# A fused attention and gMLP block on one core: w_in loaded twice in shifted row order in place of copies across partitions, with new task lists

## The chip, the core and the metric

The kernel runs on one core of a Trainium2 chip. The core has TensorE (PE in the profile; PEld is its loading of weights), VectorE (DVE), ScalarE (ACT), GpSimd (POOL) and SyncE (SP), which here only issues DMAs. The metric is the time of one execution on the device in microseconds (us). A profile shows one such execution; its span runs from the first to the last instruction, and the execution's own time is a little longer.

## The reference

Two residual blocks follow each other on 2048 tokens of 448 features, in bf16:

```python
h = x + _A_ref(_layernorm(x, axis=-1), A_wqkv, A_wo)
h2 = h + _B_ref(_layernorm(h, axis=-1), B_w_in, B_w_sp, B_b_sp, B_w_out)
```

`_A_ref` is local attention: 16 heads of 28 features; each token attends to 8 tokens, itself and those 2, 4, ... 14 positions before it. `_B_ref` is a gMLP: `z = gelu(x @ w_in)` with 1792 columns, of which the first half is z1 and the normalised second half z2; `g = w_sp @ z2 + b_sp` mixes over the tokens with a 2048 x 2048 matrix, and the output is `(z1 * g) @ w_out`.

## The kernel before

**Layout.** Tokens are cut into 16 blocks of 128. Block u and block u + 8 make unit u (u from 0 to 7) and are worked on together: after the layer norm they lie interleaved in one buffer of the ring `tring`, and a transpose puts them into `xh` as 7 chunks of 128 partitions. Partitions 0 to 63 of a chunk hold 64 features of block u, and partitions 64 to 127 the same 64 features of block u + 8. A matmul of 64 rows on the lower half and one on the upper half run side by side on PE, one for each half of the tokens. So every weight matrix that multiplies `xh` (wq, wk, wv, w_in) is needed as 7 chunks of 64 rows on both halves of the partitions.

**Where the weights come from.** A DMA on all 128 partitions puts the even chunks on one half and the odd chunks on the other. The function `cross` (used for wv and, as `cpw0`, `cpw1`, for w_in) then copies what each half lacks from the other half, on VectorE or ScalarE (the helper `copy`, lines 641 and 643). `BLK` (line 25) says for each half of the partitions which chunk of features lies in which place. wq and wk are copied into a padded form by the tasks `cpq...` and `cpk...`: 8 copies for q, 4 for k (`cpk` + first head group j, half h, parity q).

**w_in.** `ld_win(z)` loads half z of its columns (z = 1 for z2, 0 for z1) by three DMAs (256, 128 and 64 rows), and two `cross` copies follow. The readers are `mmz2_u_k` (line 984) and `mmz1_ch_f` (line 1028).

**Stages.** Layer norm 1 for each unit: `bn1_b` (statistics), `rs1_u` (reciprocal root, on POOL by lines 646 and 647 or on ScalarE by lines 668 and 669), `nrm1_b` (line 676), then a transpose, for units 7, 6, 5 on PE (`tT1_u`, line 692, with its copy `ev1_u`), for the others by a DMA (`tD1_u`, line 683). Then the projections `mmq`/`mmk` (line 783, ended by the evictions `evq`/`evk`; the first number is the stretch of tokens) and `mmv` (line 823, `evv`). Attention goes in 9 tiles i from 8 down to 0: `mml` (scores, line 858, four tasks a tile), `exp`, `mask`, `mmr` (row sums, line 886), `ln` and `rex` (reciprocal), `mmo` (line 911, four tasks), `ot`. Then `mmy_u` (line 964), the residual `h_u`, layer norm 2 (`bn2`, `rs2`, `nrm2`, and the transposes `tD2_u` by DMA), `mmz2`, its gelu `ge`, `bn3`, `ag3`, `rs3` and `nrm3` (line 1014); `mmz1` with the gelu `gz1`. The spatial matmuls `g` (line 1064) read z2 and w_sp transposed by the DMAs `wsp0_b` and `wsp1_b`; `wo` (line 1093) and stores end the kernel.

**What sets the order.** The order is written out in the file as `SEQ`, one tuple for each of SP, POOL, DVE, ACT and PE, of positions in the order in which the tasks were added. `Planner.replay` walks through these lists with estimated durations, gives out PSUM banks (eight; most matmul tasks take two, a pair, until the eviction has read them) and other buffers, and emits each engine's instructions in the order of its list. Each engine then runs its list in order and waits where something isn't ready. All DMAs but a few of the first are issued from SP's list, in order too: a transpose that waits for its input holds back what stands behind it. Each `wsp` DMA also waits until the one before it has landed (`chain`).

Decoded from the positions, PE's list up to the spatial matmuls is (`mml8_00..11` are the tasks 00, 01, 10 and 11):

```
f0 tT1_7 tT1_6 mmq3_0 mmv8 mmv7 mmq2_0 mmk3_2 mmk2_2 mmk2_0 mmk3_0 mmq3_2 mmq2_2 tT1_5 mml8_00..01 mml7_00 mml8_10..11
mml7_01 mmv6 mmq1_0 mmk1_2 mml7_10..11 mmk1_0 mmq1_2 mmr7 mmo7_0..3 mmv5 mmv2 mmr8 mmo8_0..3 mmk0_0 mmk0_2 mml6_00..01
mml5_00..01 mmq0_2 mml5_10 mml6_10 mml5_11 mml6_11 mmq0_0 mmk0_1 mmq0_3 mmr5 mmo5_0..1 mmr6 mmo5_2..3 mmq0_1 mmk0_3
mmy7 mmo6_0..3 mml4_00..11 mmv4 mml3_00..11 mmy6 mmr4 mmo4_0..3 mmv3 mml2_00..01 mmy5 mml2_10..11 mmr3 mmy4 mmo3_0..2
mmr2 mmo3_3 mmv0 mml1_00..11 mmv1 mmy3 mmr1 mmo2_0..3 mml0_00..11 mmz2_7_1 mmy2 mmo1_0..1 mmr0 mmo1_2..3 mmz2_7_0
mmz2_4_0 mmo0_0..3 mmy1 mmy0 mmz2_5_1 mmz2_5_0 mmz2_4_1 mmz1_1_0 mmz2_6_0 ... mmz1_0_1 mmz1_0_4 g0_2_0 g0_1_0 g0_0_0
```

`f0` is 15 matmuls on constants that warm PE up.

Of the kernel before, what the change touches and what calls it, by code (L numbers as in the profile page):

```python
# [23 lines left out]
DMA_T = {1: range(5), 2: range(8)}  # L24
BLK = ((0, 2, 4, 6, 1, 3, 5), (1, 3, 5, 0, 2, 4, 6))
# [353 lines left out]
def bass_sequential_preLN__sliding_local_dilated__mixer_gmlp__prompt_kernel(  # L379
# [18 lines left out]
    with contextlib.ExitStack() as top:  # L398
# [340 lines left out]

        t_cp = {}  # L740
        for p in "kq":
            for j in range(2 if p == "q" else 1):
                nh = 8 if p == "q" else 16
                for n, (h, q) in enumerate(((0, 0), (0, 1), (1, 0), (1, 1))):
                    tk = []
# [418 lines left out]
```

## Time and profile before

| | before |
|---|---|
| time, median of 3 runs | 242.88 us (242.75 to 243.28) |
| profiled execution | 242.73 us |
| its span | 240.9 us |
| PE busy | 233.1 us, 97% of the span |
| DVE, ACT, POOL busy | 140.3, 96.1, 26.9 us |
| DMA | 20.01 MB in 54628 packets |
| granted clock of PE | 1.00 throughout |

Busy time is the union of an engine's instructions in the profile. Matmuls are pipelined, so the length of one matmul is longer than the distance to the next; the price of a task on PE is best read as the distance between the starts of two tasks. In a row of the timeline the bracket gives how long the engine was idle before it and what released it; "issue" means that nothing in the profile was waited for. A row of the windows gives, for each engine, the busy time and in brackets the number of instructions.

### The profile page before, as it was taken

How to read it: one execution, taken by the hardware profiler on the slowest of the kernel's cores; microseconds unless marked ns; L12 is line 12 of the kernel's file. 1: busy time of each engine (PE TensorE's matmuls, PEld its weight loads, DVE VectorE, ACT ScalarE, POOL GpSimd, SP SyncE). 2: the span in 40 equal slices, each digit the busy share in tenths (PEclk: the TensorE clock that was granted, in tenths of full speed). 3: DMA queues.
4: the chain of work that ended last, by engine and by line, in shares of the span. 5: the costliest groups of instructions: out<-in, count | busy, mean ns of one | idle time of the engine just before them, and what ended most of it. 6: DMA issues, size and time to landing. Idle time of an engine off the chain costs nothing.

```text
span 240.9 us, 6695 instructions
## 1 busy us (share of the span) xinstructions
PE 233.1 (97%) x3009; PEld 119.9 (50%) x3019; DVE 140.3 (58%) x280; ACT 96.1 (40%) x113; POOL 26.9 (11%) x66
## 2 busy tenths in 40 slices
PE   7898999999999999999999999999999999999995
PEld 2486865456554544554444444444444444444453
DVE  5999959378999899788810050253101436554443
ACT  2996988889899947764730000000000000000000
POOL 4062000002014321304600000000000000000000
PEclk9999999999999999999999999999999999999999
DMA  7949575574213557987632733350000000010122
GB/s 213 337 106 103 112 125 95 97 127 53 44 22 77 109 85 174 169 133 117 141 76 58 174 68 65 85 46 0 0 0 3 0 0 19 20 60 0 38 93 78
DMA packets 54628, 20.01 MB, mean 83 GB/s; under 512 B 46792, under 2 KB 54472, under 8 KB 54600
## 3 DMA queue, kind: packets, MB, share of 16 engines
q1 hardware_dynamic: 53496, 18.67, 39.6%
q10 hardware_dynamic: 1104, 0.92, 1.3%
q8 instruction: 23, 0.38, 0.7%
q14 instruction: 5, 0.04, 0.1%
HBM read 6.37 MB, written 1.84 MB: 34 GB/s over the span
## 4 chain that ended last, share of the span: by engine, by line
PE 88%; DVE 5%; DMA 2%; issue 1%; POOL 1%; ACT 1%; SPq 0%
PE psum L1064 40%; PE psum L783 11%; PE psum L1093 9%; PE psum L984 8%; PE psum L964 5%; PE psum L823 5%; PE psum L1028 4%; PE psum L858 2%; PE psum L911 2%; DMA x_tm<-in_A_x_dram 2%; DVE z2p L1014 2%; PE psum L886 1%; DVE st L1000 1%; DVE tring L676 1%; POOL rs L647 1%
## 5 line engine op out<-in xcount | busy, mean ns | idle before, releaser
L1073 DVE TENSOR_TENSOR ub<-psum,reg 128x512 bf16<-128x512 f32 x28 | 18.9, 687 | 68.7 <-PE psum L1064 66.4
L1064 PE MATMUL psum<-reg,z2p 128*128 128x512 bf16 x220 | 49.4, 379 | 0.2
L1064 PE MATMUL psum<-wspT_lo,z2p 128*128 128x512 bf16 x218 | 48.5, 379 | 0.4 <-DVE z2p L1014 0.2
L1064 PEld LDWEIGHTS psum<-wspT_lo,z2p 128*128 128x128 bf16 x224 | 21.8, 98 | 26.6 <-issue 0.4
L1064 PEld LDWEIGHTS psum<-reg,z2p 128*128 128x128 bf16 x224 | 21.9, 98 | 26.2
L783 PE MATMUL psum<-xh,reg 64*128 64x128 bf16 (+2 forms) x448 | 26.0, 270 | 0.2
L1093 PE MATMUL psum<-reg 128*128 128x448 bf16 (+2 forms) x119 | 22.2, 341 | 0.1
L984 PE MATMUL psum<-w_in,xh 64*128 64x448 bf16 x224 | 22.2, 349 | 0.0
L1028 PE MATMUL psum<-xh,w_in 64*128 64x512 bf16 x196 | 21.8, 376 | 0.0
L641 ACT ACTIVATE reg<-psum 128x896 bf16<-128x896 f32 (+2 forms) x25 | 20.0, 844 | 1.9 <-PE psum L783 1.0
L783 PEld LDWEIGHTS psum<-xh,reg 64*128 64x128 bf16 x448 | 16.8, 94 | 7.8 <-issue 0.8
L656 DVE BATCH_NORM_STATS2 st<-x_tm 128x6 f32<-128x448 bf16 x32 | 19.6, 612 | 1.4 <-DMA x_tm<-in_A_x_dram 1.2
L1000 DVE BATCH_NORM_STATS2 st<-z2p 128x6 f32<-128x448 bf16 x32 | 17.5, 611 | 3.1 <-ACT z2p L994 3.1
L870 ACT ACTIVATE reg<-psum 128x928 bf16<-128x928 f32 x18 | 16.2, 939 | 4.1 <-PE psum L858 4.1
L646 POOL TENSOR_SCALAR rs<-mv 128x2 f32<-128x2 f32 x19 | 7.5, 393 | 88.4 <-DVE mv L657 70.2
L1038 ACT ACTIVATE reg<-psum 128x1024 bf16<-128x1024 f32 x14 | 13.6, 1029 | 8.0 <-PE psum L1028 8.0
L1093 PEld LDWEIGHTS psum<-reg 128*128 128x128 bf16 x119 | 11.4, 98 | 10.4
L994 ACT ACTIVATE z2p<-psum 128x896 bf16<-128x896 f32 x16 | 14.2, 916 | 5.6 <-PE psum L984 5.6
L1103 DVE TENSOR_TENSOR tring<-psum,x_tm 128x448 bf16<-128x448 f32 (+2 forms) x17 | 10.1, 596 | 10.2 <-PE psum L1093 10.1
L984 PEld LDWEIGHTS psum<-w_in,xh 64*128 64x128 bf16 x224 | 10.6, 94 | 10.4 <-issue 0.4
L929 DVE TENSOR_TENSOR reg<-psum,reg 128x912 bf16<-128x912 f32 x9 | 11.1, 1235 | 7.2 <-ACT reg L921 6.6
L1028 PEld LDWEIGHTS psum<-xh,w_in 64*128 64x128 bf16 x196 | 9.5, 94 | 11.5
(63 smaller groups left out, 205.9 us busy)
## 6 DMA issues: line engine op xcount, KB each, us to landing
x_tm<-in_A_x_dram SPq DMA_DIRECT2D x15, 112.0 KB, 4.2
out_dram<-tring SPq DMA_DIRECT2D x15, 112.0 KB, 1.7
w_in<-in_B_w_in_dram SPq DMA_DIRECT2D x2, 448.0 KB, 4.5
reg<-in_B_w_out_dram SPq DMA_DIRECT2D x1, 784.0 KB, 6.0
z2p<-in_A_wqkv_dram ACTq DMA_DIRECT2D x2, 336.0 KB, 4.5
reg<-in_B_b_sp_dram SPq DMA_DIRECT2D x1, 512.0 KB, 4.6
w_in<-in_B_w_in_dram SPq DMA_DIRECT2D x2, 224.0 KB, 4.3
reg<-in_A_wo_dram SPq DMA_DIRECT2D x4, 98.0 KB
```

The costliest lines, as they stand in the source:

```text
L641: iss("act", lambda e: e.activation(dst, src, AF.Copy), reads=rd, writes=wr)
L656: iss("dve", lambda e: e.bn_stats(st[:, b, :], x_tm[:, b, :]), reads=[r_x[b]], writes=[rl[b]])
L783: iss("pe", lambda e, c=c, s=s, gi=gi, lhs=lhs: e.matmul(psum[:, bk[s] * 512 + cw * gi:bk[s] * 512 + cw * gi + cw], lhs, xh[64 * s:64 * s ...
L870: iss("act", lambda e: e.activation(E[:, es[0], 2 * n:2 * n + 2, :], pair_view(lb, 0, 8 * JW), AF.Exp, scale=SCALE), reads=[r_bank[lb[0]], ...
L984: iss("pe", lambda e, k2=k2, c=BLK[s][k2], s=s: e.matmul(psum[:, zb[s] * 512:zb[s] * 512 + D], xh[64 * s:64 * s + 64, c, HX + 128 * u:HX + ...
L994: iss("act", lambda e: e.activation(z2p[:, u:u + 9:8, D * k:D * k + D], pair_view(zb, 0, D), AF.Gelu_apprx_tanh), reads=[r_bank[zb[0]], r_ ...
L1000: iss("dve", lambda e, b=b: e.bn_stats(st3[:, b, k, :], z2p[:, b, D * k:D * k + D]), reads=[r_z2[b][k]], writes=[r_st3[b][k]])
L1028: iss("pe", lambda e, k=k, c=BLK[s][k], s=s: e.matmul(psum[:, bk[s] * 512:bk[s] * 512 + 512], w_in[64 * s:64 * s + 64, k, 128 * f:128 * f ...
L1038: iss("act", lambda e: e.activation(z1p[f].rearrange("p (s t) -> p s t", s=2)[:, :, 512 * ch:512 * ch + 512], pair_view(bk, 0, 512), AF.Ge ...
L1064: iss("pe", lambda e, b=b: e.matmul(psum[:, gb[0] * 512:gb[0] * 512 + 512], z2p[:, b, 128 * f:128 * f + 128], src[:, b, 512 * (tc % 2):512 ...
L1073: iss("dve", lambda e: e.tensor_tensor(ub[:, us_[0], :], psum[:, gb[0] * 512:gb[0] * 512 + 512], bb[:, 512 * tc:512 * tc + 512], ALU.add), ...
L1093: iss("pe", lambda e, f=f: e.matmul(psum[:, wb[0] * 512 + d0:wb[0] * 512 + d1], z1p[f][:, 128 * m:128 * m + 128], w_out[:, f, d0:d1], star ...
```

## The change

`ld_win` now loads each half of w_in by eight DMAs, so that both halves of the partitions get all 7 chunks from memory: three loads of 128 rows from row 0, 128 and 256, three of 128 rows from row 64, 192 and 320, one of the last 64 rows onto the lower half, and one of the first 64 rows onto the upper half. The copies `cpw0` and `cpw1` are gone. The order of the chunks differs, so the two readers use a new table `BLKW`. For k, the copies of odd chunks are now made for each group of 8 heads apart (6 tasks in place of 4: cpk000 and cpk010 for all 16 heads, cpk001, cpk101, cpk011, cpk111 for 8). Three more warm-up matmuls, `f1`, follow the first transpose on PE. The planner's estimate for `rs1` on ScalarE goes from 0.36 to 0.54; that changes no instruction by itself. All five lists are new.

```diff
+BLKW = ((0, 2, 4, 1, 3, 5, 6), (1, 3, 5, 2, 4, 6, 0))
 BLK = ((0, 2, 4, 6, 1, 3, 5), (1, 3, 5, 0, 2, 4, 6))
...
-        r_win = [[Res("w_in%d_%d" % (z, n)) for n in range(5)] for z in range(2)]
+        r_win = [[Res("w_in%d_%d" % (z, n)) for n in range(8)] for z in range(2)]
...
-            parts = ((w[:, 0:2, :], src[0:256].rearrange("(m p) n -> p m n", p=128), 256, 335.0),
-                     (w[:, 2, :], src[256:384], 128, 335.0), (w[0:64, 3, :], src[384:448], 64, 154.0))
-            tl = [dma("sp", "win%d_%d" % (z, n), lambda e, dst=dst, sr=sr: e.dma_start(dst, sr), nr * FH * 2, writes=[r_win[z][n]], bw=bw)
-                  for n, (dst, sr, nr, bw) in enumerate(parts)]
-            t_win[z] = tl + cross("cpw%d_" % z, w, r_win[z], tl, FH)
+            parts = [(w[:, n, :], src[128 * (n % 3) + 64 * (n // 3):][:128], 128, 335.0) for n in range(6)]
+            parts += [(w[0:64, 6, :], src[384:448], 64, 154.0), (w[64:128, 6, :], src[0:64], 64, 154.0)]
+            t_win[z] = [dma("sp", "win%d_%d" % (z, n), lambda e, dst=dst, sr=sr: e.dma_start(dst, sr), nr * FH * 2, writes=[r_win[z][n]], bw=bw)
+                        for n, (dst, sr, nr, bw) in enumerate(parts)]
...
-                     epoch=0 if which == 1 else None, alts={"pool": 1.1, "act": 0.36} if which == 1 else None)
+                     epoch=0 if which == 1 else None, alts={"pool": 1.1, "act": 0.54} if which == 1 else None)
...
         fill("f0", 15)
+        fill("f1", 3, [pl.named["tT1_7"]])
...
-            for j in range(2 if p == "q" else 1):
-                nh = 8 if p == "q" else 16
-                for n, (h, q) in enumerate(((0, 0), (0, 1), (1, 0), (1, 1))):
+            for n, (h, q) in enumerate(((0, 0), (0, 1), (1, 0), (1, 1))):
+                whole = p == "k" and q == 0
+                for j in range(1 if whole else 2):
+                    nh = 16 if whole else 8
...
-                            iss("pe", lambda e, k2=k2, c=BLK[s][k2], s=s: e.matmul(
+                            iss("pe", lambda e, k2=k2, c=BLKW[s][k2], s=s: e.matmul(
...
-                            iss("pe", lambda e, k=k, c=BLK[s][k], s=s: e.matmul(
+                            iss("pe", lambda e, k=k, c=BLKW[s][k], s=s: e.matmul(
```

The lists decoded. PE, new:

```
f0 tT1_7 f1 tT1_6 mmq3_0 mmv8 mmv7 mmk3_0 mmq2_0 mmk2_0 mmk3_2 mmk2_2 mmq3_2 tT1_5 mmq2_2 mml8_00..11 mmq1_2 mmk1_2
mmq1_0 mml7_00..11 mmk1_0 mmv6 mmr8 mmo8_0..1 mmr7 mmo8_2..3 mmq0_3 mmq0_2 mmk0_0 mmo7_0..3 mmk0_3 mmy7 mml5_00..01
mml6_00..01 mmv5 mml5_10 mml6_10 mml5_11 mml6_11 mmq0_0 mmk0_2 mmq0_1 mmr6 mmo6_0..2 mmv4 mmo6_3 mmr5 mmk0_1 mmy6
mmo5_0..3 mml4_00..11 mmv3 mml3_00..11 mmy5 mmr4 mmv1 mmr3 mmo4_0..3 mmv2 mmo3_0..3 mml2_00..11 mmy4 mmy3 mmr2 mmv0
mml1_00..01 mmo2_0..3 mml1_10..11 mml0_00..11 mmy2 mmr1 mmz2_6_1 mmo1_0..1 mmr0 mmo1_2..3 mmz2_5_1 mmz2_6_0 mmz2_7_1
mmz2_7_0 mmo0_0..3 mmy1 mmy0 mmz2_5_0 mmz2_4_0 mmz1_1_5 ... mmz1_0_1 mmz1_0_4 g0_6_0 g1_1_0 g0_4_0 g1_3_0 g0_2_0 g1_4_0
g0_1_0 g0_0_0
```

The beginnings of the others, old and new:

```
ACT old: rs1_7 cpq011 rs1_6 cpq000 cpv1 ev1_6 cpq101 cpk001 evv8 evq3_0 evv7 evq2_0 cpq110 evk3_2 evk2_2 evk3_0 evk2_0
ACT new: rs1_7 cpq000 cpq010 ev1_7 cpq110 cpk111 cpk011 cpk000 evq3_0 evv8 evk3_0 cpk101 evq2_0 cpq100 evk2_0 evk3_2
         evk2_2 evq3_2 evv7 exp8_1 evq2_2
DVE old: bn1_6 nrm1_7 cpq001 nrm1_15 nrm1_6 cpq010 nrm1_14 ev1_7 cpv0 bn1_12 cpk010 cpk011 bn1_4 cpk000
DVE new: bn1_6 nrm1_7 nrm1_15 cpq011 cpq001 nrm1_6 nrm1_14 cpv0 cpv1 ev1_6 cpk001 cpk010 bn1_4 bn1_12
POOL old: c_wkp c_V c_ident c_eps c_wqp c_xpad c_nhalf rs1_4 c_mband rs1_5
POOL new: c_xpad c_nhalf c_eps c_ident c_wqp c_V rs1_6 c_wkp c_kpad rs1_4 rs1_5
SP old: ... x3 x8 wo0 tD1_4 x0 wo3 tD1_1 wo2 tD1_2 tD1_0 tD1_3 wsp0_7 win1_1 wsp0_15 wsp0_6 win0_2 wsp0_14 wsp0_5
        wsp0_13 win0_0 wsp0_4 tD2_7 tD2_4 tD2_5 wsp0_12 tD2_6
SP new: ... x13 x0 x10 win1_3 win1_4 wo1 x9 tD1_4 wo3 win1_6 tD1_2 tD1_3 tD1_0 tD1_1 wo0 win0_5 wsp0_7 win1_5 wo2
        wsp0_15 win1_0 win1_7 win0_4 wsp0_6 win0_6 wsp0_14 win1_2 wsp0_5 win1_1 wsp0_13 wsp0_4 tD2_6 wsp0_12 tD2_5
        tD2_7 win0_1 win0_3 wsp0_3 win0_0 win0_2 tD2_4 win0_7
```

On ACT, old, two gelus of the end stand as `ge0_1 gz1_0_6 ge1_1`; new, all `ge` tasks stand ahead of the last nine `gz1`. The new DVE list ends layer norm 3 with `nrm3_6`.

More of the change, by code (lines that the diff above doesn't have):

```diff
@@ L751, in em @@
                              w_st[p][64 * q:64 * q + 64, 0:nb, 224 * j:224 * j + nh * DH].rearrange("p c (h d) -> p c h d", d=DH),
-                             r_st[p], [r_w[p][j][n]] if p == "q" else [r_w[p][0][n], r_w[p][1][n]])
+                             r_st[p], [r_w[p][0][n], r_w[p][1][n]][j:j + nh // 8])
                     t = add("cp%s%d%d%d" % (p, j, h, q), "dve", dve4x(ne), em, deps=t_w[p] + [c_wp[p]], alts={"dve": dve4x(ne), "act": act_c(ne)})
                     tk.append(t)
-                    for jj in ((j,) if p == "q" else (0, 1)):
+                    for jj in range(j, j + nh // 8):
                         t_cp.setdefault((p, jj), []).append(t)
```

60 rows, old and new, of the table SEQ are left out of this document.

## The prediction

> **What bounds the kernel now.** I read the page's head first, then TensorE's busy time by stage, then the few places where TensorE is idle.
>
> ```profile
> span 240.9 us, 6695 instructions
> PE 233.1 (97%) x3009; PEld 119.9 (50%) x3019; DVE 140.3 (58%) x280; ACT 96.1 (40%) x113; POOL 26.9 (11%) x66
> ```
>
> TensorE (PE) is busy for 97% of the span, so the change can only move time by moving PE's idle time. Four windows, cut at the first projection, at the end of the token projections, at the last attention task and at the first spatial matmul, say where that is (length of the window, then busy time and count of PE, PEld, DVE, ACT and POOL, granted clock, DMA share, GB/s):
>
> ```profile
> 0.00:9.64 9.64, 7.08 (x29) 2.84 (x30) 7.08 (x18) 5.12 (x8) 2.73 (x15) 1.00 0.86 250
> 9.64:34.40 24.76, 23.72 (x755) 18.58 (x756) 22.03 (x49) 20.72 (x32) 5.51 (x19) 1.00 0.73 136
> 34.40:81.80 47.40, 46.39 (x1301) 25.16 (x1293) 38.02 (x56) 43.33 (x48) 5.39 (x8) 1.00 0.43 75
> 81.80:120.40 38.60, 38.53 (x379) 18.26 (x380) 34.00 (x83) 25.00 (x27) 13.23 (x24) 1.00 0.78 139
> ```
>
> Between 9.64 and 120.40 PE idles 1.04 + 1.01 + 0.07 = 2.12 us. That is all that can be won there; of the work after 120 us the change alters only the order of the first eight tasks. The timeline names the places (start, length, what, and in brackets the idle time before it):
>
> ```profile
> 1.51 5.95 PE L635 MATMUL psum<-warm 128*128 128x512 bf16 x15 [1.51 <-DVE warm L614]
> 9.04 0.56 PE L692 MATMUL psum<-ident,tring 128*128 128x128 bf16 x7 [0.56 <-DVE tring L676]
> 13.33 5.97 PE L783 MATMUL psum<-xh,reg 64*128 64x128 bf16 x196
> 21.03 0.71 PE L858 MATMUL psum<-reg 32*64 32x58 bf16 x64 [0.87 <-issue]
> 52.61 1.52 PE L823 MATMUL psum<-reg,xh 64*64 64x448 bf16 x28 [0.26 <-issue]
> 72.86 1.69 PE L964 MATMUL psum<-reg 128*128 128x448 bf16 x8 [0.75 <-DVE mv L657]
> 120.49 1.89 PE L1064 MATMUL psum<-wspT_lo,z2p 128*128 128x512 bf16 x8 [0.16 <-DVE z2p L1014]
> ```
>
> A further gap of 0.15 stands in the chain at 16.52. Windows cut inside this gap, the 0.87, the 0.26 and the 0.75 count the PE and PEld instructions between them:
>
> ```profile
> 16.52 0.15 issue
> 0.00:16.60 16.60, 13.93 (x221) 8.26 (x222) 13.80 (x32) 11.99 (x17) 5.33 (x23) 1.00 0.81 238
> 16.60:20.60 4.00, 3.50 (x127) 3.18 (x126) 3.66 (x12) 3.24 (x6) 2.19 (x7) 1.00 0.65 41
> 20.60:52.50 31.90, 31.31 (x892) 19.08 (x892) 22.26 (x35) 26.11 (x34) 0.71 (x5) 1.00 0.67 106
> 52.50:72.50 20.00, 19.50 (x638) 11.27 (x638) 19.00 (x31) 18.65 (x22) 2.70 (x5) 1.00 0.29 58
> q8 instruction: 23, 0.38, 0.7%
> ```
>
> 127 + 126 = 253, 892 + 892 = 1784 = 7 x 256 - 8, and 638 + 638 = 1276 = 5 x 256 - 4. The few that lack to multiples of 256 fit the semaphore instructions, which the page doesn't count. So all four gaps stand at boundaries in steps of 256 instructions, though the page blames the last on VectorE. Queue 8 moves 23 packets of 0.38 MB / 23 = 16.5 KB, as many as there are blocks of 256 in PE's 6028 instructions. I read the gaps as PE waiting for its own next block of code, which comes late where a block was passed quickly. They sum to 2.03 of the 2.12 us. In the Trainium skill, "Runtime: NRT & Kernel Launch", section "Instruction fetch mechanics", code comes in blocks of 256 instructions and crossing a boundary is mostly hidden. The trace agrees on the 256 and not on the cost: 0.87 us at one crossing.
>
> **The removed copies and the doubled load.** From the view of the tile w_in, from SP's waits, and from the transposes into xh:
>
> ```profile
> L643 DVE COPY w_in<-w_in x3: 1086/1087/1087, 37.3 to 81.8; 64x3584 bf16<-64x3584 bf16 x2, 64x2688 bf16<-64x2688 bf16 x1
> L641 ACT ACTIVATE w_in<-w_in x1: 2442/2442/2442, 81.5 to 81.5; 64x2688 bf16<-64x2688 bf16 x1
> L588 SPq DMA_DIRECT2D w_in<-in_B_w_in_dram x6: 454/530/1331, 7.1 to 50.2; - x6
> DMA to landing us min/median/max: 2.6/4.3/4.7
> SPq L946 <- DMA wspT_lo<-in_B_w_sp_dram: 13.9, 9, 2.1
> ```
>
> ```profile
> 17.15 1.34 SPq L683 DMA_TRANSPOSE xh<-tring  x1
> DMA to landing us min/median/max: 2.9/3.0/6.2
> ```
>
> Four copies go: 3 x 1.09 us of VectorE and 2.44 us of ScalarE. PE is busy over nearly all of that stage, so I count 0. Ten more loads are issued: 10 x 0.53 = 5.3 us of the SP queue. Most stand between the transposing loads of w_sp, where SP waits 13.9 us for landings anyway. The bytes of w_in go from 1.57 to 3.14 MB (896 rows of 1792 B for each half in place of 448); at 250 / 0.86 = 290 GB/s the difference is 5.4 us of all DMA engines, in a stage that uses 0.43 of 47 us. Again 0; without that cover, up to 5.4 us.
>
> The last load of the first half, win0_7, stands right behind the transpose tD2_4 in the queue, and the first z1 matmul, after mmz2_4_0, now waits for it. It may land up to 4.7 us after an issue that comes 1.3 us behind the transpose's, which itself needs 3.0 us; a z2 task gives 1.3 more: a wait between 0 and 1.7 us. I take 0: the old last copy of this half ended only at 81.5 + 2.44 = 84.0, and PE did not idle for it.
>
> **Start, to the first attention scores.** nrm1_15 comes before a copy in place of behind it, so the first transpose on PE comes earlier by one copy. The 3 new warm-up matmuls (f1), at 5.95 / 15 = 0.4 us each 1.2 us at the most, go into the idle 0.56 us before the second transpose, widened by that copy: 0, or some 0.25 at the slow price. rs1_6 moves from ScalarE to the slower but idle POOL; two copies now stand ahead of its reader nrm1_6: 0. Then ScalarE sets the pace:
>
> ```profile
> 6.01 0.21 ACT L669 ACTIVATE rs<-rs 128x2 f32<-128x2 f32 x1
> 8.41 1.70 ACT L641 ACTIVATE reg<-reg 64x1792 bf16<-64x1792 bf16 x1
> 10.13 0.92 ACT L641 ACTIVATE xh<-psum 128x896 bf16<-128x896 bf16 x1
> 11.07 1.97 ACT L641 ACTIVATE reg<-z2p 64x672 bf16<-64x672 bf16 x2
> 12.95 2.66 ACT L641 ACTIVATE reg<-psum 128x896 bf16<-128x896 f32 x4
> 15.63 0.95 ACT L641 ACTIVATE reg<-z2p 64x896 bf16<-64x896 bf16 x1
> 16.59 3.34 ACT L641 ACTIVATE reg<-psum 128x512 bf16<-128x512 f32 x6
> ```
>
> From 6.22 the new ScalarE list is two copies of 896 (0.95 each), ev1_7 (0.92), one more copy of 896, two of 672 (the fourth row has one of them and one of 1344 in 1.97; I take 0.76) and cpk000 with 1792 elements (1.70): 6.22 + 1.90 + 0.96 + 0.95 + 1.52 + 1.70 = 13.25. PE is free for mmk3_0 at 13.33, by the timeline, and can start at some 13.4: +0.10. Behind cpk000 come evq3_0 (0.5), evv8 (0.85; the 2.66 hold two of each), evk3_0 (0.5) and cpk101 (0.76): 15.86, so mmk3_2 starts at 16.0. Three tasks of about 0.8 (seven in 5.97) bring PE there at 15.8: +0.20, between 0 and 0.6. mmq3_2, 1.6 later at 17.6, needs a PSUM pair; evv7 is put last, so all four pairs are held until evk2_0 ends at 15.86 + 0.5 + 0.95 + 0.5 = 17.8: +0.30 with the hand-over. Sum of the waits **+0.60**, bounds 0 and 1.2.
>
> Against them stand the 0.15 and 0.87 at the first two code boundaries. The block between them, 3.50 us of work before and about as much after, now takes these waits in, so most of the gap should be covered; I leave 0.20 of 1.02: **-0.82**, bounds -1.02 and 0.
>
> If tD1_4 is issued near 17.15 again, it lands at 20.15 by the median. PE wants it at about 17.9 + 0.8 + 0.6 + 0.8 + 0.65 = 20.75 (mmq3_2, a transpose, mmq2_2, four score tasks), no longer behind mmv6 as well. tD1_1, now last in the queue, meets mmq0_3 in the same way. A wait from 0 to 1.5 us; **+0.25**, nearer the median landing than the longest.
>
> **Attention: the code blocks.** The new PE list groups the small matmuls differently. One stretch of the timeline gives the price of each kind by the distance of the starts:
>
> ```profile
> 65.26 0.71 PE L858 MATMUL psum<-reg 32*64 32x58 bf16 x64
> 65.91 1.52 PE L823 MATMUL psum<-reg,xh 64*64 64x448 bf16 x28
> 67.36 1.69 PE L964 MATMUL psum<-reg 128*128 128x448 bf16 x8
> 68.98 0.39 PE L886 MATMUL psum<-reg,ones 64*32 64x464 bf16 x8
> 69.18 0.73 PE L911 MATMUL psum<-reg 64*32 64x58 bf16 x64
> 69.85 0.83 PE L858 MATMUL psum<-reg 32*64 32x58 bf16 x64
> 70.61 1.50 PE L984 MATMUL psum<-w_in,xh 64*128 64x448 bf16 x14
> ```
>
> So four mml cost 0.65 us (128 instructions with the weight loads), mmv 1.45 (56), mmy 1.62 (16), mmr 0.20 (16), four mmo 0.67 (128), a z2 task some 1.35 (28). In the old list the blocks that ended in a gap held 3.5 us of such work (the window 16.60 to 20.60), 1.3 (mmo6 and mml4) and 2.8 (the end of mmo2, mml0, mmz2_7_1, with mmy3 and mmr1 just ahead of it); I find none without a gap below 3.6. Counting 443 instructions and then 256 at a time along the new list, these are short: the end of mmk0_1, mmy6, mmo5 and half of mml4 (2.9); the rest of mmv1, mmr3, mmo4, mmv2 (3.3); right behind it mmo3, mml2, mmy4 (2.8); the second half of mml1, mml0, mmy2, mmr1 and the start of mmz2_6_1 (3.1). Four in place of two, which cost 0.26 + 0.75 = 1.01. They cost from nothing (code asked for early, after a slow block) to 4 x 0.87 = 3.5. I take 1.6, 0.4 each, between the prices of 0.26 and 0.75, since they are less short than the old two: **+0.60**, bounds -1.01 and +2.5. PSUM pairs held long (evv0 behind exp0_1) fall into the last of them and aren't counted twice.
>
> **Start of the spatial matmuls.** g0_6_0 is now first and runs through all 16 blocks of z2 at once. The old list's last z2 gelu stood behind one of z1; the new list has all of z2's ahead, so the last nrm3 should be done: the 0.16 goes, **-0.16**. If that tail is no shorter, the 0.16 stays or doubles.
>
> Sum: +0.60 - 0.82 + 0.25 + 0.60 - 0.16 = +0.47. The profiled execution took 242.73 us (span 240.9 and 1.8 around it), 0.15 below the median of 242.88; so 243.2.
>
> **The rivals.** First, faster: boundaries cost nothing in the new order. The 2.03 and the 0.16 go, the waits of the start stay (+0.60): -1.59, so 241.1. For it: up to 120 us fourteen of eighteen boundaries show no gap. Against it: four blocks below 3.6 us. The page on the runtime in the Trainium skill, by which crossings are mostly hidden, would give this case. Second, slower: each short attention block costs what the dearest did, 0.87, at mml4_11, mmo3, mmy3 and mmz2_6_1: 3.48 - 1.60 = 1.88 more, 245.1. It decides if these gaps average above 0.65. For it: two short blocks follow each other; against it: 0.26 after a block of 1.3. Third, win0_7 is 1.0 us late at the first z1 task: 244.2; it needs the load to land after PE is through mmz2_4_0, against which speaks the 84.0 above.
>
> **How the numbers follow.** Differences below 0.2% (0.5 us) can't be told from no change. Forecast 0.42, between 242.5 and 243.9; first rival 0.31, second 0.20, third 0.07. Faster: 0.31 and a little of the forecast, 0.33. Same (242.4 to 243.4): 0.24, over half of the forecast. Slower: the rest of the forecast (0.16) and the two slow rivals (0.27), 0.43. For 8 in 10 the range goes from the middle of the first rival, 241.1, to just under the second, 244.9.
>
> **What would show it.** Gaps on PE at counts of 443 + 256 k, at the four places named; short waits before mmk3_2 and mmq3_2; none on w_in; PE's busy time unchanged. Wrong if PE's idle time between 9.6 and 120 falls to about 1 us, or if one wait for a transpose or a load of w_in exceeds 1 us.

## The result, and the profile after

The changed kernel takes 245.26 us (median of 4, 244.87 to 246.86) beside 242.81 us (242.22 to 243.28) of the kernel before: the ratio is 1.0113, with a 95% interval of 1.0077 to 1.0148. In a second set of runs, on another occasion, it was 1.0169 (1.0125 to 1.0213). The forecast was 243.2 us in a range up to 244.9; the change is slower, and by more than the range allowed. The profiled execution took 245.40 us, 2.67 more than that of before.

The head of the page of the changed kernel, the same four windows as before, and the rows of the timeline in which PE was idle first:

```profile
span 243.4 us, 6716 instructions
PE 234.5 (96%) x3012; PEld 120.5 (49%) x3022; DVE 136.9 (56%) x278; ACT 90.0 (37%) x105; POOL 29.0 (12%) x72
```

```profile
0.00:9.64 9.64, 8.13 (x50) 3.64 (x52) 7.36 (x18) 5.10 (x7) 4.97 (x21) 1.00 0.85 259
9.64:34.40 24.76, 22.16 (x645) 16.98 (x641) 18.97 (x46) 21.49 (x30) 6.75 (x20) 1.00 0.64 141
34.40:81.80 47.40, 45.78 (x1328) 25.00 (x1326) 37.81 (x56) 36.93 (x41) 5.35 (x8) 1.00 0.55 105
81.80:120.40 38.60, 38.60 (x426) 18.79 (x426) 32.66 (x83) 22.22 (x25) 11.89 (x24) 1.00 0.76 140
```

```profile
9.16 0.96 PE L785 MATMUL psum<-xh,reg 64*128 64x128 bf16 x28
...
13.16 4.27 PE L785 MATMUL psum<-xh,reg 64*128 64x128 bf16 x140 [0.27 <-ACT reg L641]
17.64 0.95 PE L785 MATMUL psum<-xh,reg 64*128 64x128 bf16 x28 [0.20 <-ACT reg L641]
32.25 4.71 PE L785 MATMUL psum<-xh,reg 64*128 64x512 bf16 x42 [2.11 <-ACT reg L923]
67.03 1.86 PE L966 MATMUL psum<-reg 128*128 128x448 bf16 x9 [0.90 <-issue]
73.14 0.45 PE L860 MATMUL psum<-reg 32*64 32x58 bf16 x32 [0.57 <-DVE reg L931]
122.99 3.19 PE L1066 MATMUL psum<-wspT_lo,z2p 128*128 128x512 bf16 x14 [0.16 <-issue]
```

In the kernel before the first projection stood later:

```profile
9.66 0.96 PE L783 MATMUL psum<-xh,reg 64*128 64x128 bf16 x28
```

So the start gained 0.50 us (9.66 to 9.16), the two gaps at the first code boundaries (0.15 and 0.87) are gone, and nothing waits for w_in. All the same the spatial matmuls begin at 122.99 in place of 120.49. The stage from 9.64 to 34.40 idles 2.60 us for 1.04, and most of that is one row: 2.11 us ahead of mmq0_3, the first projection that needs units 0 to 3, four of the five units that are transposed by DMA. The row blames ScalarE's reciprocal (L923), which ended at 30.86 + 0.98 = 31.84. What it really waited for is the transpose of unit 1, tD1_1, the second of the two transposes in this view of the line that issues them:

```profile
L683 SPq DMA_TRANSPOSE xh<-tring x2: 1300/1691/2082, 25.3 to 27.4; - x2
...
DMA to landing us min/median/max: 3.3/4.0/4.7
```

It was issued at 27.38 and took 4.7 us: it landed at 32.05, 0.20 before the matmul. The same 0.20 us lies between landing and matmul in the runs hold_loads (31.73, 31.93), lists_alone (32.19, 32.39) and after_late (30.19, 30.39) below, and in the last of them ScalarE's reciprocal ended 1.4 us after the matmul had begun.

### The profile page after: what moved, and what is told of

It reads as the page before. It is cut to its first block, busy times and chain, and to the rows that moved or that the text cites. A ratio compares the mean times of both kernels' runs of the same rounds, so it can differ in the third digit from the quotient of the medians.

```text
span 243.4 us, 6716 instructions
## 1 busy us (share of the span) xinstructions
PE 234.5 (96%) x3012; PEld 120.5 (49%) x3022; DVE 136.9 (56%) x278; ACT 90.0 (37%) x105; POOL 29.0 (12%) x72
## 4 chain that ended last, share of the span: by engine, by line
PE 92%; ACT 5%; issue 1%; DVE 1%
PE psum L1066 39%; PE psum L986 9%; PE psum L1095 9%; PE psum L1030 9%; PE psum L785 9%; PE psum L966 5%; PE psum L825 4%; ACT reg L641 4%; PE psum L635 3%; PE psum L860 2%; PE psum L913 2%; PE psum L888 1%; DVE reg L931 1%; ACT reg L923 0%; PE psum L692 0%
## 5 line engine op out<-in xcount | busy, mean ns | idle before, releaser
L641 ACT ACTIVATE reg<-psum 128x1024 bf16<-128x1024 f32 (+2 forms) x24 | 19.6, 847 | 2.5 <-PE psum L785 2.3
L931 DVE TENSOR_TENSOR reg<-psum,reg 128x912 bf16<-128x912 f32 x9 | 11.1, 1231 | 11.1 <-PE psum L913 8.4
L647 POOL TENSOR_TENSOR rs<-rs,nhalf 128x2 f32<-128x2 f32 x22 | 15.8, 719 | 1.8
```

Source lines behind the costliest of these rows:

```text
L641: iss("act", lambda e: e.activation(dst, src, AF.Copy), reads=rd, writes=wr)
L647: iss("pool", lambda e: e.tensor_tensor(dst, dst, nh, ALU.pow), reads=rr + [r_nhalf], writes=rr)
```

## The experiments

Each run has the kernel before beside it on the same chip; its median there was 242.2 to 242.6 us.

**Which part of the change costs: the load, the lists.** *loads_alone* is the kernel before with nothing but the new load:

```diff
-            t_win[z] = tl + cross("cpw%d_" % z, w, r_win[z], tl, FH)
+            parts = [...eight loads as in the changed kernel...]
 # SEQ: old lists, cpw tasks out; on SP four of the sixteen loads at the old places ahead of 20 us, twelve from 31 to 58 us
```

> The kernel before with the doubled load of w_in alone: its lists, its k copies, no f1; the four copies cpw are taken out of the lists and the 16 loads stand about where the 6 stood. The prediction's step: loads and copies lie beside PE's work, so 242.9, within 0.5 us, and PE's gaps at the same four places. Rival: 1.57 MB more make transposes or code blocks land later; then gaps grow and the time is 243.5 or more. A gain of more than 0.5 us would say that the copies had cost something.

Measured: 243.78 us (7 executions), ratio 1.0063 (1.0042 to 1.0085). The windows of two stages and the larger gaps:

```profile
9.64:34.40 24.76, 24.70 (x765) 18.99 (x761) 21.51 (x49) 21.81 (x33) 5.73 (x19) 1.00 0.68 146
34.40:81.80 47.40, 44.36 (x1276) 24.36 (x1273) 35.21 (x51) 41.27 (x46) 5.40 (x8) 1.00 0.57 101
```

```profile
52.14 1.52 PE L825 MATMUL psum<-reg,xh 64*64 64x448 bf16 x28 [1.11 <-DVE reg L931]
56.74 0.51 PE L913 MATMUL psum<-reg 64*32 64x58 bf16 x45 [0.42 <-issue]
61.56 0.33 PE L860 MATMUL psum<-reg 32*64 32x58 bf16 x17 [0.60 <-issue]
...
73.60 0.36 PE L986 MATMUL psum<-w_in,xh 64*128 64x448 bf16 x2 [0.63 <-issue]
```

The load that was to cost nothing costs 1.3 us. No row waits for w_in; the attention stage idles 3.04 us for 1.01, and all four rows stand at boundaries of 256 instructions. The stage before it idles 0.06 us for 1.04: with the old order on PE, the gaps at the first two boundaries are gone here too.

*lists_alone* is the other half, the changed kernel with the old load and its copies:

```diff
-            parts = [...eight loads...]
+            tl = [...three loads...]; t_win[z] = tl + cross("cpw%d_" % z, w, r_win[z], tl, FH)
 # SEQ: new lists; cpw1_0 and cpw1_1 on DVE behind bn2_15, cpw0_1 behind nrm2_12, cpw0_0 on ACT behind ge6_1
```

> The changed kernel with the old load of w_in (three transfers a half) and its four copies across partitions (two on VectorE in its idle time at 43 us, one each on VectorE and ScalarE at 83 and 85 us); the new lists, the changed copies of the k weights and the second warm-up stay. Theory D (the added w_in traffic makes PE's code blocks late): the load is worth the 1.3 us that it cost when it was added alone, so 243.9 to 244.3 against 245.3 of the changed kernel, and the attention gaps of 0.9 and 0.4 us shrink. Theory N (the new lists lose the time by themselves, the load's cost there being hidden): 245.0 to 245.6, with the 2.1 us gap ahead of the last q projection and the 0.9 us gap still there.

Measured: 245.56 us (6), ratio 1.0133 (1.0091 to 1.0175). The new lists alone cost as much as the whole change, and the wait for the transpose is there:

```profile
32.39 4.71 PE L787 MATMUL psum<-xh,reg 64*128 64x512 bf16 x42 [2.05 <-ACT reg L925]
56.44 0.28 PE L862 MATMUL psum<-reg 32*64 32x58 bf16 x12 [1.15 <-issue]
67.87 1.86 PE L968 MATMUL psum<-reg 128*128 128x448 bf16 x9 [0.62 <-issue]
```

So the two parts don't add up: on the old lists the load costs 1.3 us, on the new ones taking it away brings nothing that can be told (the intervals overlap). The new copies for k and the warm-up f1 are in this run too; no run parts them from the lists.

*hybrid* has the new order up to the first attention scores (on PE to mml8_11, at 21 us; layer norm 1 to its end) and the old order behind, with the new load:

```diff
 # SEQ, PE: ... mml8_11 as in the changed kernel | then the old order; mmv6 ahead of mml7_00, mmv2 behind mmo8_3
```

> The new lists up to the first attention scores (layer norm 1 to its end), the old lists behind them, with the doubled load, the new k copies and f1; mmv2 goes behind mmo8, so that the last transpose tD1_1 has time. If the start of the new lists is worth 0.8 us (first projection at 9.2 in place of 9.7, the code gaps of 0.15 and 0.87 gone, three short waits of 0.85 in all) and the loss is all behind it, the time is 242.0, below both kernels. If the start only brings forward what the rest waits for anyway, it is 242.8 or more.

Measured: 244.82 us (8, from 242.98 to 245.76), ratio 1.0074 (1.0036 to 1.0111). With the old order behind it, no projection waits for a transpose, and the earlier start is lost at two boundaries:

```profile
33.87 0.30 PE L915 MATMUL psum<-reg 64*32 64x58 bf16 x27 [1.34 <-issue]
54.86 0.21 PE L862 MATMUL psum<-reg 32*64 32x58 bf16 x2 [1.38 <-issue]
```

**The code boundaries.** *shift8* is the kernel before with eight instructions fewer ahead of everything:

```diff
-        fill("f0", 15)
+        fill("f0", 11, [c_wo0], r_wo)   # fill gets a list of reads: the first matmul waits for this memset
```

> The kernel before with four warm-up matmuls fewer (11 for 15, the first of them now waits for the memset of the weight region so that the start does not move): eight PE instructions less ahead of everything, no other edit. Theory C (idle time stands where a new block of 256 instructions is needed): the boundaries lie eight instructions later, so the blocks whose boundary fell inside a matrix product of short matmuls get a little more time; the boundary that stands before the attention matmul at 73 us (0.75 us idle in the kernel before) moves into the group behind it, so that gap shrinks to 0.1 or less, the 0.26 us one likewise, and the time is 241.4 to 242.2 against 242.8. Theory W (the gaps are data waits that the profile names issue): nothing is late for data there, the gaps stay and the time is 242.6 to 243.0.

Measured: 242.56 us (12), ratio 1.0019 (0.9996 to 1.0043): no gain, so the time that was expected is a miss. The place is as expected. In the kernel before, PE idles ahead of the 28 matmuls of mmv4; here it idles behind the first four of the same 28:

```profile
53.02 0.39 PE L824 MATMUL psum<-reg,xh 64*64 64x448 bf16 x4
53.81 1.33 PE L824 MATMUL psum<-reg,xh 64*64 64x448 bf16 x24 [0.40 <-issue]
...
57.54 0.27 PE L912 MATMUL psum<-reg 64*32 64x58 bf16 x23
58.45 0.48 PE L912 MATMUL psum<-reg 64*32 64x58 bf16 x41 [0.65 <-issue]
```

Four matmuls with their weight loads are eight instructions: the gap follows the count, not the data. The same count over the 19 profiles of these kernels, of the idle stretches of 0.30 us and more between 9.6 and 122 us, by their distance to the nearest boundary at 443 + 256 k:

```
released by, as the profile has it     stretches   within some 20 instructions ahead of a boundary
issue (nothing)                              31    29   (the others: the wait for a transpose in shift_after and busy4)
a named engine or DMA                        37     5
```

What the count does not give is the size. The boundary at mmv4 cost 0.26 us in the kernel before, 0.40 in shift8, 1.11 in loads_alone; the 0.75 us at 73 us went in shift8, and 0.65 us at 58 us came. Nor is a gap fixed to the order: of the 19 profiles only that of the kernel before has one at the first two boundaries (0.15 and 0.87 us), though loads_alone, loads_late and before_plus6 run the same old PE list there.

*loads_late* tested whether the w_in transfers make the blocks late: loads_alone with all sixteen issued later (there, twelve of them ran from 31 to 58 us, not all, as the expectation has it).

```diff
 # SEQ, SP: win1_* and win0_* out of the places from 7 to 58 us; win1_* behind wsp0_4, win0_* behind tD2_7
```

> The double load alone (243.8 when its sixteen transfers were issued from 31 to 58 us), with all sixteen issued behind the last position weights of that stage instead, from 54 us on: the same bytes, other neighbours. Theory D (a transfer of w_in that runs while a code block is fetched delays that block): the blocks fetched from 33 to 54 us come as early as in the kernel before (1.1 to 2.9 us from the asking to the fetch, against 2.4 to 4.4 with the loads there), the 1.1 us gap at 52 us goes, and what is left is at most two boundaries from 54 to 68 us: 242.6 to 243.4. Theory N (the lateness belongs to the program, not to the traffic): 243.5 to 244.1, the gap at 52 us stays.

Measured: 244.32 us (6), ratio 1.0094 (1.0066 to 1.0123). The gap at mmv4 stays though no w_in load runs near it, and one of 1.86 us appears:

```profile
52.20 1.52 PE L825 MATMUL psum<-reg,xh 64*64 64x448 bf16 x28 [0.97 <-issue]
...
73.94 0.36 PE L986 MATMUL psum<-w_in,xh 64*128 64x448 bf16 x2 [1.86 <-issue]
```

*after_late* did the same to the changed kernel:

```diff
 # SEQ, SP: the eleven win* loads ahead of wsp0_4 moved behind it (issued from 54 us)
```

> The changed kernel with the eleven w_in transfers that its SyncE queue issues from 13 to 48 us moved behind the last position weights of that stage (from 54 us, where the queue is idle until 67 us); nothing else. Theory D: the transposes of the first layer norm and the code blocks meet less traffic; the wait of 2.1 us ahead of the last q projection shrinks to 1.0 to 1.6 and the gaps of 0.9 and 0.4 us to half: 243.4 to 244.4 against 245.3. Theory N: 244.9 to 245.6 with the same gaps.

Measured: 247.52 us (6, from 245.09 to 248.68), ratio 1.0214 (1.0169 to 1.0259): slower still. Theory D, that neighbouring w_in traffic sets how late a block is, falls by both runs. In the profiled execution, the fastest of the six, the transpose was quick for once and the wait nearly gone, which the later boundaries took back (1.10 us at 62.76 and 1.04 at 66.49):

```profile
30.39 2.98 PE L787 MATMUL psum<-xh,reg 64*128 64x512 bf16 x26 [0.29 <-issue]
```

**The wait for the transpose.** *cover* moves other work in front of the waiting projection:

```diff
 # SEQ, PE:  -mmq0_3 ... mmo7_0..3 ... mmv5      +mmo7_0..3 mmv5 mmq0_3 ...       ACT: evv5 ahead of evq0_3
```

> The changed kernel with five tasks moved ahead of mmq0_3 on PE (mmo7_0..3 and mmv5, 2.0 us of work), and evv5 ahead of evq0_3 on ScalarE; nothing left out. Theory T: the 2.11 us gap before mmq0_3 is the wait for the landing of the last transpose tD1_1 (issued 27.4, landed 4.7 us later, 32.05), so the work now covers it: the gap falls to 0.1 to 0.4 us and the time by 1.7 to 2.0 us, to 243.3 to 243.6. Rival P: the page names ScalarE's rex8 as the releaser, so it is a PSUM pair or ScalarE that PE waits for; then the gap stays above 1 us and the time above 244.5.

Measured: 246.19 us (4), ratio 1.0151 (1.0115 to 1.0187): no gain. A wait of 1.33 us remains, now ahead of mmv5:

```profile
32.20 1.52 PE L827 MATMUL psum<-reg,xh 64*64 64x448 bf16 x28 [1.33 <-ACT reg L925]
```

mmv5 came behind four more small products. The row names ScalarE's reciprocal again, which frees no PSUM; the pair that mmv5 could take was free when the logarithm ahead of it had ended, at 30.88. A code boundary is five instructions further on, and that block's fetch began at 29.99. So the code block is the likelier cause, but no run parts the two; the expectation of cover2 below still speaks of PSUM.

*hold_loads* keeps wo0 and what stands behind it on SP until tD1_1 has landed:

```diff
+        t_wo[0].deps.append(t_xh[1]); t_wo[0].waits.append(t_xh[1])
```

> The changed kernel with one wait more: SP issues the load wo0, and all behind it (win0_5, the transpose wsp0_7), only when tD1_1 has landed. Theory L: these loads behind tD1_1 stretch its landing from 3.0 to 4.7 us; then it lands in 3.0 us again, the gap before mmq0_3 falls from 2.1 to 0.4 us and the time by about 1.7 us, to 243.6. Theory C: a block of PE's code, moved in between, stretches it, whatever is queued behind; then the landing stays near 4.7, the gap near 2.1, and the time at 245.3.

Measured: 247.09 us (4), ratio 1.0180 (1.0133 to 1.0226). With nothing issued behind it the transpose still took 4.69 us and PE waited 1.94: the loads behind it are not what stretches it.

What does go with the stretch is the fetch of a PE code block of 16 KB. For the 86 transposes of the first layer norm whose landing is recorded in 19 profiles, by the time from the issue to the start of the next such fetch:

```
next code fetch, us after the issue   transposes   from issue to landing, us
0 to 0.6                                  24       2.90 to 3.75
0.6 to 1.1                                 9       6 take 3.24 to 3.54, 3 take 4.52 to 4.78
1.1 to 2.3                                 6       4.43 to 4.68
2.3 to 2.8                                19       5 take 2.91 to 3.02, 14 take 4.60 to 4.77
2.8 and more, or none                     28       2.88 to 3.15
```

From 2.3 to 2.8 us both lengths occur, so the distance alone does not decide it there.

*shift_after* moves that fetch by 14 instructions; the shorter warm-up, as it turned out, is followed by a lower clock of PE as well:

```diff
-        fill("f0", 15)
-        fill("f1", 3, [pl.named["tT1_7"]])
+        fill("f0", 10)
+        fill("f1", 1, [pl.named["tT1_7"]])
```

> The changed kernel with 10 warm-up matmuls for 15 in the first task and 1 for 3 in the second: 14 PE instructions fewer ahead of everything, nothing else moved. In the ten profiles so far a transpose of the first layer norm whose issue is followed by the fetch of a PE code block 0.75 to 2.65 us later landed after 4.4 to 4.8 us in 13 of 17 cases, and after 2.9 to 3.5 us in all 28 others. Theory F (the fetch holds up the transpose): the block that was fetched 2.59 us after the issue of the last transpose is now fetched some 0.35 us later, 2.9 to 3.0 us after it, the transpose lands after 3.0 us instead of 4.7, PE's wait falls from 2.1 to 0.3-0.6 us, and the time is 243.4 to 244.4. Theory G (the transpose is slow for its place in the queue or for the loads around it): it still takes 4.7 us, the wait is 1.9 to 2.2 us, 245.0 to 245.6.

Measured: 247.32 us (6), ratio 1.0161 (1.0110 to 1.0211). The fetch came 3.5 us after the issue, and the transpose was quick:

```profile
L685 SPq DMA_TRANSPOSE xh<-tring x1: 1299/1299/1299, 30.2 to 30.2; - x1
...
DMA to landing us min/median/max: 3.0/3.0/3.0
```

PE's wait fell to 0.62 us, as theory F had it. The time did not follow: behind the shorter warm-up PE ran at half its clock from 8 to 15 us, which put everything later, and again from 59 to 63 us. So this is one profile in which the fetch was moved and the transpose was quick, beside the table; in shift_cover2 below the last transpose is quick too (2.96 us), with a fetch 2.61 us behind its issue. The fetch is the likely cause of the stretch, not a proven one.

*cover2* moves mmv5 alone, without the four small products:

```diff
 # SEQ, PE:  -mmq0_3 ... mmv5 mml5_10      +mmv5 mmq0_3 ... mml5_10       ACT: evv5 ahead of evq0_3
```

> The changed kernel with one v projection (1.5 us, 28 matmuls) and its eviction moved ahead of the q projection that waits 2.1 us for the last transpose; the four short attention products stay behind it this time, so the spot needs neither a new code block nor the pair of PSUM banks that the run with five tasks moved waited for. Theory T (this wait is time on the path): 1.5 of the 2.1 us are filled, 0.5 to 0.7 us are left, and the time is 243.6 to 244.4. Theory R (what is gained there is lost again further on, at the code blocks and ScalarE's evictions of the attention stage): 245.0 or more.

Measured: 244.88 us (6), ratio 1.0098 (1.0061 to 1.0135), beside 247.06 us of the changed kernel in the same set:

```profile
30.07 1.52 PE L827 MATMUL psum<-reg,xh 64*64 64x448 bf16 x28
32.29 4.06 PE L787 MATMUL psum<-xh,reg 64*128 64x512 bf16 x36 [0.69 <-ACT reg L925]
...
121.94 4.26 PE L1068 MATMUL psum<-wspT_lo,z2p 128*128 128x512 bf16 x19 [0.16 <-issue]
```

The wait is 0.69 us for 2.11, and the spatial matmuls begin at 121.94 for 122.99: of the 1.42 us gained here 1.05 reach them in the profile. So this wait is time on the path. The times can't give the size: the whole is 2.2 us faster by the medians, but four of the six executions beside it are among the long ones that are taken up below, and the first set's ratio of the changed kernel, 1.0113, lies inside the interval of cover2. *shift_cover2* has both edits:

> Both edits together. If both causes are right they fill the same wait, so together they bring little more than the better of the two: no wait left ahead of that projection and 243.2 to 244.0. If the gain is lost again behind it (theory R): 244.8 or more.

Measured: 245.41 us (6), ratio 1.0147 (1.0101 to 1.0193). No wait is left ahead of that projection in the profile, and the total is no better than cover2 alone, again with PE's clock halved in the shortened warm-up.

**The spread of the executions.** *after_again* is the changed kernel once more.

> The changed kernel itself once more, beside the next three on the same chip. Every theory: 245.0 to 245.6 us, the wait of about 2.1 us ahead of the last group of q projections again.

Measured: 247.06 us (6), ratio 1.0169 (1.0125 to 1.0213). Together with the first set, its ten executions lie at 244.9 to 245.4 us (five) and at 246.7 to 247.7 us (five). The profile of the one at 247.67 us has its last two stores land late, with the fetch of a 24th code block (the other profile has 23) between their issue and their landing:

```profile
q8 instruction: 24, 0.39, 0.6%
```

```profile
L1110 SPq DMA_DIRECT2D out_dram<-tring x2: 333/382/430, 241.7 to 242.1; - x2
...
DMA to landing us min/median/max: 3.2/3.3/3.4
```

In the first profile of the changed kernel the same two stores took:

```profile
DMA to landing us min/median/max: 1.6/1.6/1.6
```

hold_loads shows 3.3 and 3.1 us with such a fetch; in lists_alone, though, the last store took 2.6 us without one. I took this for the cause of the upper group and tested the six instructions that the change adds to PE's list: *after_minus6* takes them out, *before_plus6* adds six to the kernel before, *cover2_minus6* takes them out of cover2.

```diff
 # after_minus6, cover2_minus6
-        fill("f0", 15)
+        fill("f0", 12, [c_wo0], r_wo)
 # before_plus6, behind the 15 matmuls of f0
+                for _ in range(3):
+                    iss("pe", lambda e: e.matmul(psum[:, fb[0] * 512:fb[0] * 512 + 32], warm[:, 0:128], warm[:, 0:32]), ...)
```

> The changed kernel with 12 warm-up matmuls for 15, the first waiting for the memset of the weight region so that the warm-up ends where it did: six PE instructions fewer, as many as the kernel before has (6038 for 6044 by the lists). In the profiles so far a 24th PE code block of 16 KB was fetched at the very end in 4 of 8 kernels with 6044 instructions and in none of 6 with 6038 or fewer; in the two where it fell between the last stores' issue and their landing, these two took 3.4 and 3.2 us for 1.6. Theory E (the six added instructions bring that last fetch into the stores' window): no 24th fetch before the stores have landed, no run in the upper group (246.7 to 247.7 us), all runs 244.4 to 245.5. If the transpose is let through as well (its block is fetched 0.1 to 0.2 us later), 1.7 us less. Theory S (the two groups are the chip's, with the instruction count no part of it): runs in both groups again, median 245 to 247.

> The kernel before with three tiny warm-up matmuls (32 columns) added to the first task: six instructions more, 6044 as in the changed kernel. Theory E: some of its runs, a third to two thirds, are 1.5 to 1.8 us longer (243.6 to 244.4 for 242.0 to 242.8), with the last two stores landing after more than 3 us in a profile of such a run. Theory S: no second group; 242.2 to 242.9 as before, but for the gaps at code boundaries, which move by six instructions (plus or minus 0.4).

> The run with one v projection moved ahead of the waiting q projection (244.88, 243.49 to 245.94), with the same six instructions fewer. Theory E with the transposes' wait: the upper half of its runs goes, 243.3 to 244.3. Theory S: 244.4 to 245.4.

Measured: after_minus6 246.93 us (6, from 246.02), ratio 1.0191 (1.0164 to 1.0219); before_plus6 242.90 (12), ratio 1.0023 (0.9997 to 1.0050); cover2_minus6 244.73 (6), ratio 1.0097 (1.0070 to 1.0124). The upper group stays without the six instructions: theory E falls as the cause of all of it. With them the kernel before has two long executions of twelve (245.29 and 244.74), but their spans are 242.2 and 241.7 us; what is long there is the time around the span, 3.1 and 3.0 us. The late stores stay the difference in the profile of 247.67 us, whose clock is 1.00. The profiles show a second cause. In after_minus6, behind the wait for the transpose, and in cover2_minus6, behind a wait for a PSUM pair, the granted clock (third number from the end) is halved:

```profile
32.41 0.82 PE L787 MATMUL psum<-xh,reg 64*128 64x512 bf16 x6 [2.21 <-ACT reg L925]
```

```profile
32.40:33.60 1.20, 1.19 (x12) 0.68 (x14) 0.83 (x1) 0.00 (x0) 0.00 (x0) 1.00 0.77 191
33.60:37.00 3.40, 3.40 (x20) 1.46 (x16) 0.00 (x0) 2.48 (x3) 0.00 (x0) 0.50 0.73 155
37.00:40.00 3.00, 3.00 (x87) 1.53 (x84) 0.37 (x1) 1.35 (x2) 0.00 (x0) 1.00 0.81 215
```

```profile
71.41 0.44 PE L862 MATMUL psum<-reg 32*64 32x58 bf16 x32 [0.61 <-DVE reg L933]
```

```profile
71.80:75.20 3.40, 3.40 (x24) 1.12 (x16) 2.96 (x5) 2.04 (x3) 0.00 (x0) 0.53 0.66 126
```

3.4 us at half clock are 1.7 us of work lost, and take 0.7% from the mean clock of the execution. A mean clock below 0.996 was recorded in 1 of 71 executions of the kernel before, in 3 of the 10 of the changed kernel (three of the five in its upper group; the other two, 246.86 and 247.67, have 1.00), in 5 of 6 of after_minus6, and in none of the 25 of loads_alone, loads_late and before_plus6, which have the old lists (in 2 of 12 of shift8, whose profile has it behind the shortened warm-up, from 9 to 12.6 us). In the Trainium skill, "TensorE: Matmul & The Clock Gate", section "The HAM clock gate", PE's clock has two states, full and half, decided over a free-running window of about 3.4 us; these rows agree on both numbers. By the page it takes an idle window of that length to fall to half; here 2.21 us of idle time, and once 0.61, stood ahead of a fall. The measurement decides: the clock can fall without an idle stretch of that length, in some executions.

Last, *busy8* and *busy4* keep the wait for the transpose and fill it with matmuls:

```diff
+                        for _ in range(8 if p == "q" and t0 == 0 and g0 == 3 else 0):   # busy4: 4
+                            iss("pe", lambda e: e.matmul(psum[:, bk[0] * 512:bk[0] * 512 + 512], warm[:, 0:128], warm[:, :]), ...)
```

> The changed kernel with eight warm-up matmuls (128x512, 0.216 us each, operands long there, into the PSUM bank that the next product overwrites) put right ahead of the q projection that waits 2.1 us for the last transpose: the wait stays, but PE is busy in 1.7 of its 2.1 us. Theory H (an idle stretch of about two microseconds makes the clock gate halve PE's clock for about 3.4 us in some of the executions, 1.7 us of time each): no execution with a mean granted clock of 0.993 any more, the times keep to the lower group, 244.7 to 245.7, median 245.1 or less. Theory J (the clock falls for the short attention matmuls or by the chip, with the wait no part of it): a third to a half of the executions stay at 0.993 and 246.5 to 248.

> The same with four warm-up matmuls: PE is busy in 0.9 of the 2.1 us and idle for 1.2. Theory H: between the changed kernel and the run with eight, 0 to 2 of 6 executions in the upper group. Theory J: as the changed kernel, a half in the upper group.

Measured: busy4 245.48 us (6, all between 244.90 and 245.82, all at clock 1.00), ratio 1.0124 (1.0101 to 1.0147); busy8 248.73 us (6), ratio 1.0255 (1.0216 to 1.0294), four of them at 0.993. The row of busy4 after the four matmuls:

```profile
29.95 1.04 PE L782 MATMUL psum<-warm 128*128 128x512 bf16 x4
31.84 0.39 PE L788 MATMUL psum<-xh,reg 64*128 64x512 bf16 x2 [0.85 <-issue]
```

busy4 is what theory H expects, busy8 is the contrary. Its one profile has clock 1.00 throughout and so doesn't show where the others lost it. So it is shown that the clock falls in many executions with the new lists. In the 19 profiles three falls begin behind the first projection (in after_minus6, cover2_minus6 and shift_after), each 0.6 to 1.2 us behind the end of an idle stretch; that this one wait is what draws them is not shown.

No kernel of these beats the kernel before.

## Why the prediction was wrong

Step by step, by its own sum, with what the profiled execution of the changed kernel shows for it (spatial matmuls 2.50 us later than before):

- **The start.** Not in the sum: the first projection begins 0.50 us earlier.
- **Waits at the start, +0.60.** Right. Rows of 0.27 and 0.20 us stand where they were put (mmk3_0 and mmq3_2, for ScalarE's copies and evictions); from start to start of the single tasks, mmk3_0, mmk3_2 and mmq3_2 are 0.32, 0.17 and 0.36 us longer than their price: 0.85.
- **The first two code gaps, -0.82.** Near by number: both are gone, -1.02. The reason given, that waits take in the block between them, is not shown and may be luck: both are gone in loads_alone, loads_late and before_plus6 as well, with the old order on PE.
- **The transposes, +0.25.** This is the step that failed. The prediction named the place (tD1_1, last in the queue, meets mmq0_3), priced it by the median landing of 3.0 us, and set the bound at 1.5. It took 4.7 us, and the wait was 2.11, 1.86 more than the term, of the 2.0 us by which the sum falls short; the other misses nearly cancel. In cover2's profile most of what is taken off this wait reaches the spatial matmuls. The view of that line in the kernel before gave 2.9/3.0/6.2 as minimum, median and maximum over all DMA transposes; two of its own five transposes of this stage had taken 4.5 and 4.6 us, each with a code fetch 1.2 us behind its issue. One is tD1_4, issued at 17.15, which the prediction let land at 20.15: it landed at 21.60. The other is the last of the row in the old list, in the view below. The bound should have come from these.
- **The attention blocks, +0.60 for four short ones against two.** About right as a sum, wrong one by one: 0.90 us ahead of mmy4 and about 0.4 behind mml4_11, and nothing at mmo3 and mmz2_6_1. That is 1.3 us for 1.01 of before, +0.3. The 0.57 us ahead of mml0_10 stands half a block from any boundary: by its row it is a wait for the VectorE task of L931, which frees a PSUM pair, and it stood at 0.40 to 0.64 us in every profile with the new attention order. The prediction had folded it into a code gap that did not come; it is 0.6 to 0.9 us more.
- **The start of the spatial matmuls, -0.16.** Wrong: the row still shows 0.16.

-0.50 + 0.85 - 1.02 + 2.11 + 0.3 + 0.75 (the middle of 0.6 to 0.9) is 2.5 us, the distance seen. The last transpose of the row in the kernel before, by the view of its line:

```profile
L683 SPq DMA_TRANSPOSE xh<-tring x1: 1220/1220/1220, 29.6 to 29.6; - x1
...
DMA to landing us min/median/max: 4.6/4.6/4.6
```

**The load at nothing.** On the old lists it costs 1.3 us, though no row ever waits for w_in and win0_7 landed at 87.2, ahead of its reader at 89.6. The cover that was named, idle DMA engines and SP's own waits, covered the bytes and not what came with them: more idle time at code boundaries. Moving the loads in time did not bring it back (loads_late), and no run on the old lists changed the bytes alone, so how the load does it stays open. On the new lists it made no difference that was measured.

**The rivals.** The time is near that of the second, 245.1, but not for its reason: boundaries cost 1.3 us, not 3.5. The first, that boundaries cost nothing, is out: 29 of 31 stretches of 0.30 us and more in which PE waited for nothing stand at crossings, 0.34 to 1.86 us long. The sentence of the Trainium skill, "Runtime: NRT & Kernel Launch", section "Instruction fetch mechanics", that crossings are mostly hidden agrees with these traces by count alone: 34 of some 340 crossings between 9.6 and 122 us in the 19 profiles show such a stretch. The third did not happen. The prediction's own test for being wrong, a wait above 1 us for a transpose, is what came true. What no step held is the fall of PE's clock, 1.7 us in each execution that has it; none of the four executions of the first set does (0.999 to 1.00), so it has no part in the 245.26 us.

## What to carry to other kernels

When PE is full for 97% of the time, a new order is priced by its largest single wait: look for the first matmul that needs the last of a row of DMAs, and bound its wait by the slowest landing in the profile, not by the median. One long job that is ready, with few instructions, covered such a wait here (cover2, 1 us in the profile); many tiny matmuls there bring the next code boundary forward, which is the likelier reason why cover gained nothing. Idle time that PE shows with no releaser should be counted in instructions before it is put down to data.

## What the runs showed of the hardware

- DMA transposes of the first layer norm with a fetch of a 16 KB code block 1.1 to 2.3 us behind their issue took 4.4 to 4.7 us in 6 of 6 cases, and 2.9 to 3.2 us in all 28 with the next fetch 2.8 us and more behind it, or none; in between both occur. The two last stores took 3.2 and 3.4 us in place of 1.6 in an execution where such a fetch came among them. That the fetch is what holds them up is likely and not proven.
- PE's granted clock was halved for 3.4 us behind idle stretches of 2.21, 1.86 (shift_after, at 58 us) and 0.61 us, far less than the 3.4 us themselves, and stayed full behind others of that size. A fall costs 1.7 us, a part of the 2.9 us between the shortest and the longest execution of the changed kernel (244.87 and 247.72).
- The time around the span was 1.8 to 1.9 us in all 71 executions of the kernel before, and 2.4 to 3.3 us in five of the thirteen of loads_alone and loads_late, two of the twelve of before_plus6 and one each of after_minus6, cover2_minus6 and hold_loads. Nothing here explains it.
